# Opening of a fused FFT and feed-forward kernel: first sequence's loads on two queues, its stores and first reads on others

## Chip, core and metric

The kernel runs on one core of one Trainium2 chip. The metric is the device time of one execution in microseconds, the median of several runs. Before the change it is 2823.06 us (3 runs, 2822.7 to 2823.41).

## What is computed

The input x has 8 sequences of 3008 rows with 256 channels, in float32. Each sequence is transformed, mixed, soft-thresholded and transformed back; all 24064 rows then pass a gated feed-forward layer:

```python
X = np.fft.rfft(x, axis=1)
Yr = Xr @ w_r - Xi @ w_i + b_r
Yi = Xr @ w_i + Xi @ w_r + b_i
Y  = soft(Yr, 0.01) + 1j * soft(Yi, 0.01)      # sign(v) * max(|v| - 0.01, 0)
y  = np.fft.irfft(Y, n=3008, axis=1)
out = (sigmoid(y @ w_gate) * (y @ w_val)) @ w_out    # 256 -> 1536 -> 256
```

## The kernel before

The transform of 3008 = 47 x 64 points is made in two steps. Step A (`fwd_a`) takes 47-point transforms. A sequence is cut into 8 units `xf` of 96 rows x 1024 floats (384 KB); a unit is loaded (`load_a`), multiplied in two halves of 512 columns with the constant `fa_sb` (`product_a`, tile `pa`), copied from the PSUM bank back over the unit and stored (`store_a`) to a scratch tensor `zd` in DRAM. Of the two copies of a unit, ScalarE makes the first and VectorE the second while the sequence is 0 or 1. Step B (`load_b`, `fwd_b`) reads `zd` back in 12 pieces q of 256 KB (`zf`), and each piece needs rows of all 8 units, so none can be read before the last unit of its sequence has been stored. `fwd_b` multiplies it with a table `mf_sb` (`pb`), `mix4` multiplies with the mixing weights (`pm`), `inv_b` goes back with a table `mi_sb` (`pi`), and the result is stored to `vd`. The steps of three successive q are interlaced: round q makes `pb` of q, `pm` of q-1, `pi` of q-2.

Only sequence 0 is computed with nothing beside it; its opening is written out by hand (lines 853 to 914) under a manual schedule, so every engine takes its instructions in program order. Ahead of the first unit and again ahead of the first `pb`, TensorE runs matmuls on zeros (`keep_warm`, tile `warm`, L830): 13 and 10 of them. Between, step A runs for the 8 units of sequence 0 and for the first 4 (`EARLY`) of sequence 1. Later sequences are transformed beside the feed-forward layer, which fills most of the program.

All plain transfers of this opening are issued by SP (`nc.sync`), except the load of `fa_sb`, which ACT issues first; POOL (`nc.gpsimd`) issues the stores to `vd`. Transfers that SP and ACT issue take eight completion semaphores in turn, DMAHW0 to DMAHW7, in program order over both engines. A transfer that gets a semaphore a second time waits, on its issuing engine, until the transfer that held it before has landed. POOL's transfers have eight of their own (DMASW0 to DMASW7). Three PSUM banks hold `pa` and `pb`.

Of the kernel before, what the change touches and what calls it, by code (L numbers as in the profile page):

```python
# [19 lines left out]
R2, R1 = 47, 64  # L20
NK2 = 24
NQ = 2 * NK2
# [10 lines left out]

LAST_GAP, SIDE_GAP = 20, 3
PRE = 2
WARM = 13
WARM_Z, WARM_V = 10, 5
EARLY = 4
AT_FIRST = 3
NCONV = 7  # L40
# [69 lines left out]
def tile_fft_mix_ffn(ctx: ExitStack, tc, x, w_r, w_i, b_r, b_i, w_one, w_out, mf, mi, mis, fa, fb, out):  # L110
    nc = tc.nc
# [3 lines left out]
    XR = x.shape[2]  # L115
# [25 lines left out]
    def bank(name, tag="fft", bufs=FFT_BANKS):  # L141
        return (psf if tag == "fft" else psl).tile([P, 512], F32, tag=tag, bufs=bufs, name=name)
# [10 lines left out]
    zd = [tc.dram_tile([NQ, R1, D], F32, name=f"zd{b}") for b in range(B)]  # L153
# [4 lines left out]
    xv = x.rearrange("b u p (h c) -> b u p h c", c=D)  # L158
# [7 lines left out]
    def big(name):  # L166
        return p2.tile([P, 4, D], F32, tag="big", bufs=NBIG, name=name)

    def load_a(b, h):
        xf = p0.tile([P, 4, D], F32, name="xf0", bufs=R1 // 8) if b == 0 else big("xf")  # L170
        nc.sync.dma_start(xf[:XR], xv[b, h])
        held["x", b, h] = xf

    def product_a(xi, az, copy):
        pa = bank("pa")[:2 * NQ]
        nc.tensor.matmul(pa, fa_sb, xi, start=True, stop=True)  # L176
        copy(az, pa.rearrange("p (h c) -> p h c", h=2))  # L177

    def fwd_a(b, h):

        xf = held["x", b, h]
        for i in range(2):
            at = slice(2 * i, 2 * i + 2)
            product_a(xf[:2 * R2, at], xf[:2 * NQ, at], nc.vector.tensor_copy if b < 2 and i else nc.scalar.copy)

    def store_a(b, h, queue=nc.sync):
        queue.dma_start(zv[b][:, 4 * h:4 * h + 4], held.pop(("x", b, h))[:2 * NQ])

    def load_half(b, h):
        xf = r2k("xfh").bitcast(F32)  # L190
        nc.sync.dma_start(xf[:XR], xv[b, h // 2, :, h % 2 * 2:h % 2 * 2 + 2])
        held["xh", b, h] = xf
# [9 lines left out]
    def load_mf(q):  # L202
        t = p2.tile([P, 2, P], F32, name="mf_sb", bufs=NMF)
        nc.sync.dma_start(t, mf[2 * q:2 * q + 2].rearrange("q p k -> p q k"))
        return t
# [18 lines left out]
        nc.gpsimd.dma_start(md[2 * q:2 * q + 2].rearrange("q p a k -> p q a k"), t.bitcast(F32))  # L224
        kept.add(q)

    def load_b(b, q):
        zf = p2.tile([P, 2, D], F32, tag="ld", bufs=NLD, name="zf")
        nc.sync.dma_start(zf, zd[b][4 * q:4 * q + 4].rearrange("(q a) n c -> (a n) q c", q=2))
        held["z", b, q] = zf  # L230

    def fwd_b(b, q, m, full):
        zf = held.pop(("z", b, q))
        pb = bank("pb").rearrange("p (c q k) -> p c q k", c=CT, q=2)
        for i in range(2):
            for ct in range(CT):
                nc.tensor.matmul(pb[:, ct, i], zf[:, i, ct * P:(ct + 1) * P], m[:, i], start=True, stop=True)  # L237
        xh, xl = (p2.tile([P, CT, 3, 2 * R1], F32R, tag=t, name=t) for t in ("xsh", "xsl"))
        if full:

            xh, xl = (t.rearrange("p c s k -> p c (s k)").rearrange("p c (q k) -> p c q k", q=2) for t in (xh, xl))
            nc.scalar.copy(xh[:, :, :, 64:], pb)
            sub(xl[:, :, :, 64:], pb, xh[:, :, :, 64:])
            for t in (xh, xl):
                nc.scalar.mul(t[:, :, :, :64], t[:, :, :, 128:], -1.0)
        else:

            xf = p2.tile([P, CT, 3, 2, R1], F32, name="xsf", bufs=1)
            nc.scalar.copy(xf[:, :, 0:2].rearrange("p c t q k -> p c q t k"),
                           pb.rearrange("p c q (t k) -> p c q t k", t=2))  # L250
            nc.vector.tensor_add(xf[:, :, 2], xf[:, :, 0], xf[:, :, 1])
            flat = xf.rearrange("p c s q k -> p c s (q k)")
            nc.scalar.copy(xh, flat)
            sub(xl, flat, xh)
        held["xs", b, q] = xh, xl
# [490 lines left out]
    def load_mix():  # L746
        for w in (w_r, w_i):
            wf = f2k("wf")
            nc.sync.dma_start(wf, w.rearrange("(t p) d -> p t d", p=P))
            wfs.append(wf)  # L750

    def load_bias4():
        for i, v in enumerate((b_r, b_i)):
            nc.sync.dma_start(bias4[64 * i:64 * i + 64], v.rearrange("(o d) -> o d", o=1).broadcast_to([64, D]))

    def load_bias():
        for i, v in enumerate((b_r, b_i)):
            nc.sync.dma_start(bias_sb[:, i], v.rearrange("(o d) -> o d", o=1).broadcast_to([P, D]))

    def mix_weights():  # L760
        wi = p0.tile([P, CT, 2, D], F32R, tag="xf0", bufs=R1 // 8, name="wi_sb")
        nc.scalar.copy(wi[:, :, 0], wfs[1])
        sub(wi[:, :, 1], wfs[1], wi[:, :, 0])
        wd, wn = f2k("wd"), f2k("wn")
        sub(wd, wfs[1], wfs[0])
        nc.vector.scalar_tensor_tensor(wn, wfs[0], -1.0, wfs[1], op0=ALU.mult, op1=ALU.subtract)
        for i, w in enumerate((wfs[0], wd, wn)):
            nc.scalar.copy(w_sb[:, :, 0, i], w)
            sub(w_sb[:, :, 1, i], w, w_sb[:, :, 0, i])
        return wi  # L770
# [24 lines left out]
    def load_part():  # L795
        k, f = parts.pop(0)
        if len(parts) >= 3 * NF // 2 - NCONV:
            raw = p0.tile([P, 2, D, 2], U32, tag="xf0", bufs=R1 // 8, name="raw0")
        else:
            raw = p2.tile([P, 2, D, 2], U32, tag="big", bufs=NBIG, name="raw")  # L800
        nc.sync.dma_start(raw.rearrange("p i n w -> p (i n w)"), (w_out[f // 2] if k else w_one[f]).bitcast(U32))
        raws.append((k, f, raw))
# [24 lines left out]
    def keep_warm(o, l, r, n):  # L827

        for _ in range(n):
            nc.tensor.matmul(o, l, r, start=True, stop=True)  # L830

    keep_warm(bank("warm"), zero[:, :P], zero, WARM)
    tables = {}
# [5 lines left out]
    mfs, mis_ = {}, {}  # L839
# [13 lines left out]
    with tc.manual_schedule():  # L853
        for h in range(na):
            load_a(0, h)
        load_a(1, 0)
        for h in range(na):
            fwd_a(0, h)
            store_a(0, h)
            if h in (1, 3, 4):  # L860
                load_a(1, {1: 1, 3: 2, 4: 3}[h])
            if h == 2:
                load_mix()
        mfs[0] = load_mf(0)
        for q in range(2):
            load_b(0, q)
        mfs[1] = load_mf(1)
        load_bias4()
        load_part()
        mfs[2] = load_mf(2)  # L870
        for h in range(EARLY):
            fwd_a(1, h)
            if h == 1:
                wi_sb = mix_weights()
        keep_warm(bank("warm"), zero[:, :P], zero, WARM_Z)
        for q in range(NP + 2):
            if q + 2 < NP:
                load_b(0, q + 2)
            if 0 <= q - 1 < NP:
                mis_[q - 1] = load_mi(q - 1, True)  # L880
            if q < 2:
                for h in range(q * EARLY // 2, (q + 1) * EARLY // 2):
                    store_a(1, h)
            if q == 3:
                nc.sync.dma_start(fb_sb, fb)
                load_bias()
            if q % 2 and q <= NP:
                load_part()
            if q % 2 == 0 and 4 <= q < 4 + 2 * (na - EARLY):
                load_a(1, EARLY + q // 2 - 2)  # L890
            if q < NP:
                fwd_b(0, q, mfs[q], True)
            if q + 3 < NP:
                mfs[q + 3] = load_mf(q + 3)

            if q % 2:
                ops("sum word", 0)
                start_part(p0)
                ops("exp top", -1)
            elif q:  # L900
                ops("power mant", -1)
                if len(started) > 1:
                    ops("hi lo", 0)
                ops("one", -1)
            if q == 4:
                sub(bias_sb[:, 1], bias_sb[:, 1], bias_sb[:, 0])
            if 0 <= q - 1 < NP:
                mix4(0, q - 1)
            if q == NP + 1:

                fwd_a(1, EARLY)
                store_a(1, EARLY, nc.gpsimd)
            if 0 <= q - 2 < NP:
                inv_b(0, q - 2, mis_[q - 2], True)

        for bh in beside[:NR2K]:
            load_half(*bh)
        left = ["hi lo", "power mant one", "sum word", "hi lo"]
        for h in range(EARLY + 1, na):
            ops(left.pop(0), 0)  # L920
            fwd_a(1, h)
            store_a(1, h, nc.gpsimd)
        ops(left.pop(0), 0)
# [46 lines left out]
    n = len(a3) // 3  # L970
# [13 lines left out]
    for j in range(NF, len(ffn)):  # L984
        c, f = divmod(j, NF)
# [46 lines left out]
    with tc.manual_schedule():  # L1032
# [16 lines left out]
        n = NPR * NH  # L1049
# [36 lines left out]
```

## Time and profile before

| | |
|---|---|
| median of 3 runs | 2823.06 us |
| the profiled execution, its own time | 2821.45 us |
| its span, first to last instruction | 2819.6 us |
| TensorE (PE) busy | 2802.0 us, 99% |
| VectorE (DVE) / ScalarE (ACT) / GpSimd (POOL) busy | 74% / 46% / 25% |
| data moved by the 16 DMA engines | 241.01 MB, mean 85 GB/s |

The profiled execution has a span of 2819.6 us and a time of 2821.45 us, so 1.85 us lie outside of the span. PE is the matmul engine, PEld its weight loads. SPq, ACTq and POOLq are the sequencers that issue transfers. The 40 slices of the page show the DMA engines busy in the first two fifths of the program and hardly afterwards.

### The profile page before, as it was taken

What the parts mean: (1) busy time and instruction counts of PE and PEld (TensorE: products, weight loads), DVE (VectorE), ACT (ScalarE), POOL (GpSimd) and SP (SyncE); (2) the same over time, 40 slices, a digit from 0 to 9 for tenths busy, and PEclk for the clock granted to TensorE, in tenths of its full rate; (3) what the DMA queues carried; (4) which work ended last, traced back from release to release, by engine and by line L of the source; (5) the groups of instructions that cost most, each with busy time, mean ns of one, the idle gap of its engine ahead of it and who ended that gap; (6) DMA issues with size and microseconds to landing.
All of it is one profiled execution on the core that took longest, in us unless ns stands there. A gap on an engine that the chain in (4) does not pass through costs nothing.

```text
span 2819.6 us, 38247 instructions
## 1 busy us (share of the span) xinstructions
PE 2802.0 (99%) x13896; PEld 2307.9 (82%) x13896; DVE 2082.6 (74%) x3109; ACT 1309.8 (46%) x2276; POOL 711.7 (25%) x638
## 2 busy tenths in 40 slices
PE   9999999999999999999999999999999999999999
PEld 6778888888899887888888888888888888888887
DVE  5778778667787536777777777777777777777776
ACT  4664544544455444444444444444444444444443
POOL 0211010224100002333333333333333343333321
PEclk9999999999999999999999999999999999999999
DMA  9866545656554661000000000000000000000000
GB/s 295 265 214 190 172 138 156 200 180 191 163 156 144 185 182 36 30 15 16 30 31 24 7 31 31 31 16 15 31 30 16 15 30 31 30 1 30 30 16 16
DMA packets 173469, 241.01 MB, mean 85 GB/s; under 512 B 14592, under 2 KB 124896, under 8 KB 173280
## 3 DMA queue, kind: packets, MB, share of 16 engines
q1 hardware_dynamic: 163776, 214.93, 24.9%
q0 software_dynamic: 9408, 23.60, 2.5%
q8 instruction: 110, 1.80, 0.3%
q14 instruction: 79, 0.65, 0.1%
q10 hardware_dynamic: 96, 0.04, 0.0%
HBM read 134.17 MB, written 104.33 MB: 85 GB/s over the span
## 4 chain that ended last, share of the span: by engine, by line
PE 95%; DVE 2%; DMA 2%; ACT 0%; issue 0%; SPq 0%; DVEq 0%; ACTq 0%
PE pd L653 11%; PE pc L653 11%; PE pa L653 11%; PE po L630 8%; PE po L629 8%; PE po L628 8%; PE pm L271 6%; PE pb L653 5%; PE pia L340 4%; PE pa L176 3%; PE pb L237 3%; PE pg L395 2%; PE pg L397 2%; PE po L420 2%; PE pg L396 2%; PE po L421 2%
## 5 line engine op out<-in xcount | busy, mean ns | idle before, releaser
L630 PE MATMUL po<-hl,w 128*128 128x512 f32 x912 | 362.7, 398 | 0.0
L629 PE MATMUL po<-hh,w 128*128 128x512 f32 x912 | 361.7, 397 | 0.0
L628 PE MATMUL po<-hh,w 128*128 128x512 f32 x912 | 360.9, 396 | 0.0
L712 POOL TENSOR_TENSOR c<-c,c 128x512 f32<-128x512 f32 x114 | 147.7, 1296 | 833.5 <-DVE c L708 613.4
L653 PE MATMUL pc<-s,w1h 128*128 128x512 f32 x912 | 284.1, 393 | 1.4 <-DVE v L687 1.4
L653 PE MATMUL pa<-a,w1h 128*128 128x512 f32 x912 | 284.1, 393 | 0.0
L708 DVE TENSOR_TENSOR c<-u,pc 128x512 f32<-128x512 f32 x228 | 156.7, 687 | 114.7 <-PE pc L653 106.3
L683 DVE TENSOR_TENSOR u<-u,pb 128x512 f32<-128x512 f32 x228 | 155.3, 681 | 91.1 <-PE pb L653 64.1
L600 ACT CAST hh<-v 128x512 fp32r<-128x512 f32 x114 | 70.7, 620 | 306.0 <-DVE v L693 306.0
L630 PEld LDWEIGHTS po<-hl,w 128*128 128x128 f32 x912 | 171.5, 188 | 41.9
L628 PEld LDWEIGHTS po<-hh,w 128*128 128x128 f32 x912 | 172.1, 189 | 40.9
L629 PEld LDWEIGHTS po<-hh,w 128*128 128x128 f32 x912 | 171.1, 188 | 40.7
L653 PEld LDWEIGHTS pa<-a,w1h 128*128 128x128 f32 x912 | 171.2, 188 | 40.1
L653 PEld LDWEIGHTS pc<-s,w1h 128*128 128x128 f32 x912 | 170.9, 188 | 39.5 <-DVE v L687 2.3
L604 POOL TENSOR_TENSOR hl<-c,hh 128x512 fp32r<-128x512 f32 x114 | 152.6, 1338 | 186.1 <-ACT hh L600 186.1
L271 PE MATMUL pm<-w_sb,xsh 128*128 128x256 f32 x1008 | 189.4, 288 | 1.4 <-ACT xf L177 1.1
L653 PE MATMUL pc<-s,w1l 128*128 128x512 f32 x456 | 177.6, 389 | 0.0
L653 PE MATMUL pa<-a,w1l 128*128 128x512 f32 x456 | 177.0, 388 | 0.0
L685 DVE TENSOR_TENSOR v<-u,pd 128x512 f32<-128x512 f32 x228 | 156.8, 688 | 25.0 <-DVE u L683 0.9
L714 DVE TENSOR_TENSOR u<-u,pd 128x512 f32<-128x512 f32 x228 | 156.9, 688 | 24.4 <-DVE c L708 0.9
L687 DVE TENSOR_TENSOR v<-v,pc 128x512 f32<-128x512 f32 x228 | 156.6, 687 | 24.1 <-DVE v L685 0.5
L679 ACT COPY u<-pa 128x512 f32<-128x512 f32 x228 | 133.7, 586 | 81.6 <-PE pa L653 81.6
(166 smaller groups left out, 6739.6 us busy)
## 6 DMA issues: line engine op xcount, KB each, us to landing
zf<-zd SPq DMA_DIRECT2D x96, 256.0 KB, 3.5
vf<-vd SPq DMA_DIRECT2D x128, 192.0 KB, 3.2
out_dram<-ot SPq DMA_DIRECT2D x93, 256.0 KB, 2.2
vd<-vz SPq DMA_DIRECT2D x84, 256.0 KB, 2.9
ypair<-yd SPq DMA_DIRECT2D x19, 1024.0 KB, 5.0
yd<-yf SPq DMA_DIRECT2D x103, 188.0 KB, 3.1
xf<-in_x_dram SPq DMA_DIRECT2D x48, 384.0 KB, 4.2
zd<-xf SPq DMA_DIRECT2D x44, 384.0 KB, 3.6
```

The costliest lines, as they stand in the source:

```text
L271: nc.tensor.matmul(o, l, r, start=(i == 0), stop=(i == len(mms) - 1))
L604: sub_(hl, h, hh)
L628: nc.tensor.matmul(o, wh, hh, start=(f == 0), stop=False)
L629: nc.tensor.matmul(o, wl, hh, start=False, stop=False)
L630: nc.tensor.matmul(o, wh, hl, start=False, stop=(f == NF - 1))
L653: nc.tensor.matmul(o, l, r, start=not more and l is wh and r is xh, stop=l is wl, skip_group_check=more)
L683: add(u, u, b)
L685: add(v, u, d)
L687: add(v, v, c)
L708: add(c12, u, c)
L712: nc.gpsimd.tensor_mul(c12, g12, c12)
L714: add(u, u, d)
```

## The change

Sequence 0's units are now loaded as two halves of 192 KB (512 columns each), the first issued by SP, the second by ACT. Of the two copies of a unit of sequence 0, VectorE now makes the first and ScalarE the second; sequence 1 keeps its order. The stores of sequence 0's units are issued by ACT, each right behind ACT's copy of that unit. The first two reads `zf` are issued by POOL. The loads of sequence 1's units 1, 2, 3 stand after units 1, 4, 6 of sequence 0 (before 1, 3, 4), and the first `mf` table after unit 5 (before after unit 7). The fourth unit of sequence 1 passes step A after the first `pb` instead of ahead of the second group of `warm`, and the four stores of sequence 1 stand one in each of rounds 0 to 3 instead of two in each of rounds 0 and 1. The `warm` groups have 10 and 5 matmuls.

```diff
-WARM = 13
-WARM_Z, WARM_V = 10, 5
+WARM = 10
+WARM_Z, WARM_V = 5, 5
...
     def load_a(b, h):
         xf = p0.tile([P, 4, D], F32, name="xf0", bufs=R1 // 8) if b == 0 else big("xf")
-        nc.sync.dma_start(xf[:XR], xv[b, h])
+        if b == 0:
+            for i, queue in enumerate((nc.sync, nc.scalar)):
+                queue.dma_start(xf[:XR, 2 * i:2 * i + 2], xv[b, h, :, 2 * i:2 * i + 2])
+        else:
+            nc.sync.dma_start(xf[:XR], xv[b, h])
...
-            product_a(xf[:2 * R2, at], xf[:2 * NQ, at], nc.vector.tensor_copy if b < 2 and i else nc.scalar.copy)
+            product_a(xf[:2 * R2, at], xf[:2 * NQ, at], nc.vector.tensor_copy if b < 2 and i == b else nc.scalar.copy)
...
-    def load_b(b, q):
+    def load_b(b, q, queue=nc.sync):
...
-        nc.sync.dma_start(zf, zd[b][4 * q:4 * q + 4].rearrange("(q a) n c -> (a n) q c", q=2))
+        queue.dma_start(zf, zd[b][4 * q:4 * q + 4].rearrange("(q a) n c -> (a n) q c", q=2))
...
-            store_a(0, h)
-            if h in (1, 3, 4):
-                load_a(1, {1: 1, 3: 2, 4: 3}[h])
+            store_a(0, h, nc.scalar)
+            if h in (1, 4, 6):
+                load_a(1, {1: 1, 4: 2, 6: 3}[h])
...
-        mfs[0] = load_mf(0)
+            if h == 5:
+                mfs[0] = load_mf(0)
         for q in range(2):
-            load_b(0, q)
+            load_b(0, q, nc.gpsimd)
...
-        for h in range(EARLY):
+        for h in range(EARLY - 1):
             fwd_a(1, h)
...
-            if q < 2:
-                for h in range(q * EARLY // 2, (q + 1) * EARLY // 2):
-                    store_a(1, h)
+            if q < EARLY:
+                store_a(1, q)
...
             if q < NP:
                 fwd_b(0, q, mfs[q], True)
+            if q == 0:
+                fwd_a(1, EARLY - 1)
```

ACT's rows at the start of the program, before. `fa_sb` is step A's constant, `xf_123` unit 0 and `xf_125` unit 1 of sequence 0; what stands behind "waits" are semaphores, DMAHW those of transfers:

```order
1 L151 DMA fa_sb<-in_fa_dram 94x96
2 L177 ACT_TABLE_LOAD [waits DMAHW1_49]
3 L177 COPY xf_123<-pa 96x512 [waits PE_49]
4 L177 COPY xf_125<-pa 96x512 [waits DMAHW2_49,PE_49]
5 L177 COPY xf_127<-pa 96x512 [waits DMAHW3_49,PE_49]
```

ACT's rows at the same place now, where `xf_120`, `xf_123`, `xf_126`, `xf_129` are units 0 to 3 and `zd_77` is sequence 0's scratch tensor:

```order
3 L173 DMA xf_123<-in_x_dram 96x512
4 L173 DMA xf_126<-in_x_dram 96x512
5 L173 DMA xf_129<-in_x_dram 96x512 [waits DMAHW0_49]
6 L173 DMA xf_132<-in_x_dram 96x512 [waits DMAHW2_49]
7 L173 DMA xf_135<-in_x_dram 96x512 [waits DMAHW4_49]
8 L173 DMA xf_138<-in_x_dram 96x512 [waits DMAHW6_49]
9 L173 DMA xf_141<-in_x_dram 96x512 [waits DMAHW0_49]
10 L181 ACT_TABLE_LOAD
11 L181 COPY xf_120<-pa 96x512 [waits PE_49]
12 L191 DMA zd_77<-xf_120 96x1024 [waits DMAHW3_49,DVE_49,Activation_49]
13 L181 COPY xf_123<-pa 96x512 [waits PE_49]
14 L191 DMA zd_77<-xf_123 96x1024 [waits DMAHW6_49,DVE_49,Activation_49]
```

Eight loads now stand ahead of ACT's first copy, five of them with a wait for an earlier transfer, and a store stands behind each copy. In the last load DMAHW0 is that of unit 3's second half.

SP's rows around the last stores of sequence 0, before (`xf<-in_x_dram` are units of sequence 1, `wf` the mixing weights):

```order
13 L187 DMA zd_77<-xf_127 96x1024 [waits DMAHW5_49,DVE_49,Activation_49]
14 L749 DMA wf<-in_w_r_dram 128x2x256 [waits DMAHW6_49]
15 L749 DMA wf<-in_w_i_dram 128x2x256 [waits DMAHW7_49]
16 L187 DMA zd_77<-xf_129 96x1024 [waits DMAHW0_49,DVE_49,Activation_49]
17 L171 DMA xf<-in_x_dram 96x1024 [waits DMAHW1_49]
18 L187 DMA zd_77<-xf_131 96x1024 [waits DMAHW2_49,DVE_49,Activation_49]
19 L171 DMA xf<-in_x_dram 96x1024 [waits DMAHW3_49]
20 L187 DMA zd_77<-xf_133 96x1024 [waits DMAHW4_49,DVE_49,Activation_49]
21 L187 DMA zd_77<-xf_135 96x1024 [waits DMAHW5_49,DVE_49,Activation_49]
22 L187 DMA zd_77<-xf_137 96x1024 [waits DMAHW6_49,DVE_49,Activation_49]
23 L204 DMA mf_sb<-in_mf_dram 128x2x128 [waits DMAHW7_49]
24 L229 DMA zf<-zd_77 128x2x256 [waits DMAHW5_49,DMAHW4_49,DMAHW6_49,DMAHW2_49,DMAHW0_49]
```

SP's rows there now; `raw_222` is a piece of the feed-forward weights, and the `zf` in row 21 is the third one:

```order
10 L175 DMA xf<-in_x_dram 96x1024 [waits DMAHW2_49]
11 L753 DMA wf<-in_w_r_dram 128x2x256 [waits DMAHW4_49]
12 L753 DMA wf<-in_w_i_dram 128x2x256 [waits DMAHW5_49]
13 L175 DMA xf<-in_x_dram 96x1024 [waits DMAHW7_49]
14 L208 DMA mf_sb<-in_mf_dram 128x2x128 [waits DMAHW0_49]
15 L175 DMA xf<-in_x_dram 96x1024 [waits DMAHW2_49]
16 L208 DMA mf_sb<-in_mf_dram 128x2x128 [waits DMAHW3_49]
17 L758 DMA bias_98<-in_b_r_dram 64x256 [waits DMAHW4_49]
18 L758 DMA bias_98<-in_b_i_dram 64x256 [waits DMAHW6_49]
19 L805 DMA raw_222<-in_w_one_dram 128x1024 [waits DMAHW7_49,DVE_49,Activation_49]
20 L208 DMA mf_sb<-in_mf_dram 128x2x128 [waits DMAHW1_49]
21 L233 DMA zf<-zd_77 128x2x256 [waits DMAHW4_49,DMAHW3_49,DMAHW5_49,DMAHW2_49,DMAHW0_49]
```

SP's list has lost the stores: loads that stood behind a store, or behind the first `zf`, now stand ahead of it. By the order of issue the semaphores pair the stores on ACT with these loads: the store of unit 2 waits for the landing of sequence 1's unit 0, that of unit 3 for `w_i`, of unit 4 for the first `mf`, of unit 5 for sequence 1's unit 3, of unit 6 for the second `mf`, and that of unit 7 for `b_r` (row 17). Behind the rounds of the opening the five engines have the same instructions in the same order as before.

## Rows read from the trace of the kernel before

**Rows 1.** Busy time by stretch of the span, with granted clock and DMA.
```profile
core 0: us, PE busy (x) PEld busy (x) DVE busy (x) ACT busy (x) POOL busy (x), PEclk, DMA share, GB/s
0.00:40.00 40.00, 34.81 (x120) 18.84 (x121) 15.71 (x26) 13.87 (x24) 0.20 (x4) 1.00 0.91 281
40.00:80.00 40.00, 39.63 (x311) 38.48 (x311) 33.99 (x59) 25.32 (x47) 6.00 (x8) 1.00 0.98 300
120.00:2819.60 2699.60, 2689.41 (x13293) 2224.49 (x13291) 2004.52 (x2975) 1247.18 (x2163) 696.02 (x610) 1.00 0.25 77
```
**Rows 2.** PE in order of time: start, us, instruction, idle before and its releaser.
```profile
1.46 4.98 PE L830 MATMUL warm<-zero 128*128 128x512 f32 x13 [1.46 <-DVE ebias L838]
6.28 17.49 PE L176 MATMUL pa<-xf,fa_sb 94*96 94x512 f32 x40
...
28.10 2.77 PE L830 MATMUL warm<-zero 128*128 128x512 f32 x10
31.88 1.13 PE L237 MATMUL pb<-mf_sb,zf 128*128 128x128 f32 x8 [1.02 <-issue]
...
38.97 1.13 PE L237 MATMUL pb<-mf_sb,zf 128*128 128x128 f32 x8 [1.52 <-DMA zf<-zd]
...
47.90 1.10 PE L305 MATMUL pi<-yc,mi_sb 128*128 128x256 f32 x4 [0.37 <-DMA mi_sb<-in_mi_dram]
```
**Rows 3.** The chain that ended last, 0 to 140 us: start, us, what.
```profile
21.47 7.49 DMA zd<-xf
...
32.83 6.00 DMA zf<-zd
...
49.00 0.89 PE pb L237 x8
49.89 2.84 PE pm L293 x24
```
**Rows 4.** SP's queue in order of time: start, us, transfers issued.
```profile
0.74 5.91 SPq L171 DMA_DIRECT2D xf<-in_x_dram  x9
...
29.04 0.89 SPq L229 DMA_DIRECT2D zf<-zd  x2
```
**Rows 5.** SP's waits, 0 to 60 us: total, times, longest.
```profile
SPq L171 <- DMA fa_sb<-in_fa_dram: 1.9, 1, 1.9
```
**Rows 6.** ACT in order of time, first rows; columns as in rows 2.
```profile
5.18 1.28 ACT L177 ACT_TABLE_LOAD   x1 [5.18 <-DMA xf<-in_x_dram]
7.33 0.58 ACT L177 COPY xf<-pa 96x512 f32<-96x512 f32 x1 [0.87 <-PE pa L176]
```
**Rows 7.** The transfers of the first 28.5 us in sum.
```profile
DMA packets 3118, 8.54 MB, mean 300 GB/s; under 512 B 461, under 2 KB 1198, under 8 KB 3118
```
**Rows 8.** Four stretches; columns as in rows 1, DMA rate last.
```profile
5.00:14.00 9.00, 9.00 (x24) 3.85 (x23) 2.56 (x4) 3.61 (x5) 0.00 (x0) 1.00 1.05 263
16.00:28.00 12.00, 11.28 (x27) 3.71 (x25) 6.94 (x11) 6.18 (x11) 0.00 (x0) 1.00 1.03 388
...
88.00:91.00 3.00, 3.00 (x15) 2.04 (x14) 2.81 (x6) 1.27 (x2) 0.42 (x1) 1.00 0.94 326
104.00:109.00 5.00, 4.38 (x26) 3.57 (x26) 2.32 (x5) 2.77 (x5) 0.00 (x0) 1.00 1.02 397
```
**Rows 9.** DMA queues, 104 to 109 us: packets, MB, share of 16 engines.
```profile
q1 hardware_dynamic: 504, 1.00, 53.4%
q0 software_dynamic: 303, 0.98, 48.6%
```
**Rows 10.** POOL's stores to vd, 40 to 100 us: ns min/median/max, times, landing.
```profile
L313 POOL DMA_DIRECT2D vd<-vz x12: 725/725/902, 44.7 to 94.4; - x12
...
DMA to landing us min/median/max: 2.6/5.4/7.7
```
**Rows 11.** Warm matmuls on PE, 2.1 to 5 us and 29.2 to 30.4 us: ns, starts.
```profile
L830 PE MATMUL warm<-zero x8: 628/628/795, 1.5 to 4.6; 128*128 128x512 f32 x8
...
L830 PE MATMUL warm<-zero x7: 389/389/394, 28.9 to 30.2; 128*128 128x512 f32 x7
```

## The prediction

> **What bounds the kernel now.** First I read the stretches. Behind 120 us TensorE is busy for 2689.41 of 2699.60 us, and the instructions there don't change; so the change can only move the moment at which that work begins [rows 1]. From 40 to 80 us PE is busy for 39.63 of 40 us too. The loss lies in the first 40 us, where PE is busy for 34.81 us, warm matmuls among them, while the DMA engines are at 0.91 [rows 1].
>
> Then I read PE in order of time. The reader is to see four losses: `pa` begins at 6.28 us; after step A there are 2.77 us of `warm` and 1.02 us of nothing, until the first `pb` at 31.88; the third `pb` waits 1.52 us for `zf` and begins at 38.97; a `pi` waits 0.37 us for a table [rows 2]. From there PE runs without a gap worth naming, so what counts is the time at which the third `pb` starts, plus the 0.37 us.
>
> The chain says what sets it: the store of the last unit, issued at 21.47 us, takes 7.49 us and lands at 28.96; then SP issues the first two `zf` [rows 3, 4]. The third `zf` is issued at 32.83 and takes 6.00 us, behind other loads [rows 3]. So the opening hangs on DMA: how many bytes stand ahead of the last store, and how fast they move. In 28.5 us 8.54 MB moved, 300 GB/s [rows 7]. That rate has two parts: from 5 to 14 us, units of x alone, 263 GB/s; from 16 to 28 us, loads and stores mixed, 388 GB/s; the DMA share is 1.0 in both [rows 8].
>
> **The change part by part.** The sum is made against the profiled execution's own 2821.45 us, 1.61 us under the median of 2823.06.
>
> *Warm matmuls.* At full pace one follows another in 0.22 us (seven from 28.9 to 30.2) [rows 11]. Three fewer let `pa` begin at 6.28 - 0.66 = 5.62 us, if its data are there. `fa` landed at about 5.85: SP's nine issues end at 6.65, the last two took some 0.4 us each, and the wait for `fa` ended right before them [rows 4, 5]. So `pa` gains 0.4 to 0.66 us; it is not on the path, since the last store is late for other reasons (below), and counts 0. Five fewer ahead of `pb` lie in the wait for `zf` and count 0 too. The price if the cover fails: after idling, the eight first warm matmuls took 628 ns where later ones took 389, 8 x 0.24 = 1.9 us [rows 11]. I take 0, since gaps of 1.02 and 1.52 us left the two `pb` groups behind them at 1.13 us each [rows 2].
>
> *ACT as a queue.* An issue costs (5.91 - 1.9) / 9 = 0.45 us [rows 4, 5]. Eight of them would delay ACT by 3.6 us, but the fourth waits for `fa` (5.85 us) and the eighth for the landing of the fourth. Unit 3 is 1.5 MB into the stream; at 263 GB/s, from about 2 us, with 1.5 to 2 us to land, that is 9.5 to 10 us. Then comes the table load, 1.28 us, so ACT's first copy comes at about 11.5 instead of 7.33 us [rows 6]. PE makes five products of 0.87 us (17.49 / 20) until 10 us [rows 2], and then stalls some 2 us for a bank that ACT has not emptied. This lies beside the x loads, which run until 14 us anyway, and counts 0 as long as DMA sets the last store.
>
> *Bytes ahead of the last store.* Before: 12 units of x and 8 stores at 384 KB, `wf` 512 KB, `fa` 35 KB, together 8.42 MB. Now the store of unit 7 can't be issued before `b_r` lands, and ahead of that stand two `mf` (128 KB each) and `b_r` (64 KB): 0.33 MB more, 0.85 us at 388 GB/s. Up to 0.72 MB more (`b_i`, `raw`, a third `mf`), issued by SP without a store before them, can share the engines with the last stores: 2.7 us in all. Between 0.85 and 2.7 I take 1.8.
>
> *Two queues for x.* The 3.15 MB of sequence 0 took 12.0 us at 263 GB/s. Halves of a unit, in rows of 2 KB and almost alone, moved at 326 GB/s from 88 to 91 us; two queues, half loads and half stores, at 397 from 104 to 109 [rows 8, 9]. That makes 12.0, 9.6 or 7.9 us: a gain from 0 to 4.1. The nearest row is the 326, but there SP alone issued the loads; I take half of its 2.4 us, 1.2. The Trainium skill (DMA: Bandwidth & Descriptors, section Rules for kernel authors) speaks against this term: spreading transfers over SP, ACT and GpSimd doesn't help bandwidth, since all run on the same 16 DMA engines and interleave. The 397 of two queues beside the 388 of one agrees with it for mixed traffic; for loads alone no row here decides. By that rule this term is 0 and the sum 1.2 us higher.
>
> *Stores in ACT's order.* A store waiting for its semaphore now holds up ACT's next copy, and so the bank that PE needs. The store of unit 5 leaves when sequence 1's unit 3 has landed. Behind it two more rounds of copy (0.58) and issue (0.45) follow, about as long as a store's own transfer (0.39 MB at 388 GB/s, 1.0 us). I take a bubble of 0.5 us, within 0 to 1.5.
>
> The last store then lands at 28.96 + 1.8 - 1.2 + 0.5 = 30.1 us.
>
> *First two `zf` by POOL.* Before: from issue at 29.04 to `pb` at 31.88, 2.84 us [rows 2, 4]. POOL takes 0.73 to 0.90 us to issue 256 KB, and its stores land 2.6 us after the start in quiet, 5.4 in the median [rows 10]. The third `zf`, now issued by SP at the same moment, shares the engines. I take 3.6 us, 0.75 more; bounds -0.2 and +2.5.
>
> *From first to third `pb`.* Before, 38.97 - 31.88 = 7.09 us. Now: `pb` 0.89, the fourth unit of sequence 1 (two products, 1.74), `pb` 0.89, `pm` 2.84 [rows 2, 3], together 6.36, if the third `zf` is there; it no longer stands behind `raw` and the biases. -0.75, with +0.9 if it is late. The wait of 0.37 us ahead of `pi` goes as well, since that table is asked for earlier relative to PE: -0.37, or 0.
>
> Sum: 1.8 - 1.2 + 0.5 + 0.75 - 0.75 - 0.37 = +0.73 us, from 2821.45 to 2822.2 in a profiled execution; on the median, 2823.06 + 0.73 = 2823.8 us. All lower ends together give 0.85 - 4.1 + 0 - 0.2 - 0.75 - 0.37 = -4.6 us, all upper ends 2.7 - 0 + 1.5 + 2.5 + 0.9 + 0 = +7.6 us.
>
> **The rivals.**
>
> *The two queues pay in full.* If loads alone go at the 397 GB/s of two queues, sequence 0 has landed at about 11 instead of 15 us; ACT's first copy comes near 9.5; the last store lands near 26, PE idles less, and the time is about 2823.06 - 4 = 2819.1. For it: 263 GB/s is far under what the same engines moved later at the same share of 1.0 [rows 8]. Against it: PE's own 16 products take 14 us and end near 20 at the earliest, and more bytes stand ahead of the last store.
>
> *ACT's queue becomes the bound.* Place: the stores of units 2 to 7, each held until a load of SP's queue has landed, with ACT's copies, PE's banks and the next stores behind it. Price: no gain from the queues, 2.7 us of bytes, a 1.5 us bubble, a late `zf` (+0.75 to +2.5) less 0.75 to 1.1: about +5 us, 2828. It decides from the point at which the last store lands after 31.5 us. For it: the waits in the order; before, a store waited only for loads issued long before. Against it: in the chain before, the engines were never idle until 28 us, so a held store gives its time to a load that has to be moved anyway.
>
> *The fewer warm matmuls cost.* If the longer stalls slow what follows, 1.9 us are added to the forecast; it lies within the range and is counted with the second rival.
>
> **How the numbers follow.** Forecast (-1.5 to +2.5 us): 0.55; two queues pay: 0.25; ACT the bound: 0.20. The likeliest gives 2823.8 us. Forecasts of both signs hold much of the chance, so the likeliest one's own range is 2821.6 to 2825.6; the range for 8 in 10 takes in most of both rivals, 2819.3 to 2827.8. About what a measurement of this kernel can tell from no change is 0.2%, 5.6 us. Only the tails beyond the rivals' own prices reach that: 0.06 faster and 0.06 slower, 0.88 within.
>
> **What would show it.** Right: the DMA rate over the first 14 us above 263 but under 330 GB/s; ACT's first copy after 10 us and a PE stall of about 2 us ahead of the sixth product; the last store of `zd` landing at 30 us, the first `pb` at 33 to 34, the third at about 39.7 with no wait for `zf` ahead of it, and from there every row of PE at a constant shift. Wrong: a last store that lands under 28 or over 32 us; a first copy of ACT at 8 us; `pm` beginning late because the mixing weights, which ACT now casts behind its last store, are not ready; or PE rows behind 120 us whose shift is not that of the third `pb`.

## The result and the profile after

The changed kernel takes 2836.91 us (median, 2835.29 to 2839.07), the kernel before 2822.88 in the same runs: the ratio is 1.0049, with an interval of 1.0037 to 1.0061. It is slower, by 14 us (0.5%); forecast was +0.7, within 2819.3 to 2827.8. The profiled execution took 2837.03 us, 15.6 more than that of before.

First the stretches of the changed kernel; columns as in [rows 1].

```profile
0.00:40.00 40.00, 35.25 (x50) 12.58 (x50) 7.01 (x12) 8.13 (x13) 1.84 (x6) 0.67 0.87 260
...
6.00:13.00 7.00, 4.86 (x12) 1.43 (x10) 2.06 (x3) 1.86 (x2) 0.00 (x0) 1.00 1.07 258
14.00:47.00 33.00, 31.38 (x41) 10.44 (x40) 9.10 (x14) 7.39 (x13) 1.64 (x2) 0.50 0.70 228
48.00:60.00 12.00, 12.00 (x92) 10.82 (x91) 8.05 (x14) 7.62 (x15) 0.73 (x1) 1.00 0.82 251
```

In [rows 1] PE does 120 matmuls in the first 40 us, here 50, and is just as busy: 35.25 against 34.81 us. Busy time hides the loss; the clock column shows it. TensorE's granted clock is at its upper level (2.4 GHz) until 13 us, at the lower one (1.2 GHz) from 14 to 47 us, and at the upper one again from 48.

PE in order of time, the changed kernel; columns as in [rows 2].

```profile
1.46 4.63 PE L834 MATMUL warm<-zero 128*128 128x512 f32 x10 [1.46 <-DVE ebias L842]
5.89 4.93 PE L180 MATMUL pa<-xf,fa_sb 94*96 94x512 f32 x10
12.96 22.16 PE L180 MATMUL pa<-xf,fa_sb 94*96 94x512 f32 x26 [2.14 <-ACT xf L181]
...
43.15 3.12 PE L834 MATMUL warm<-zero 128*128 128x512 f32 x5
46.33 1.69 PE L241 MATMUL pb<-mf_sb,zf 128*128 128x128 f32 x8
...
53.30 1.06 PE L241 MATMUL pb<-mf_sb,zf 128*128 128x128 f32 x8
```

Ten passes (five products) take 4.93 us; then PE waits 2.14 us for ACT; the next 26 passes take 22.16 us, 0.85 each instead of the 0.44 of [rows 2]. The third `pb` starts at 53.30 instead of 38.97 us. That is 14.3 us of the 15.6; the first matmul of the next stage (tile `po`) is 14.7 us late, and the end 15.6. The prediction expected one constant shift behind the third `pb`; 1.3 us more arise there. The medians differ by 14.0 us only, and executions of the kernel before lie from 2820.86 to 2826.34 us (those beside e9), so the 1.3 may be spread.

The chain that ended last, the changed kernel, 0 to 140 us; columns as in [rows 3].

```profile
4.56 6.10 DMA xf<-in_x_dram
...
10.68 0.32 ACTq L173
...
11.03 0.44 ACT L181
...
12.33 0.59 ACT xf L181
...
12.96 22.18 PE pa L180 x26
...
46.33 1.69 PE pb L241 x8
```

Before, the chain ran over the last store and the read of it [rows 3]. Now it goes from a load of x to ACT's last issue, through ACT's table load and first copy, into PE's slow passes.

ACT in order of time, the changed kernel, the rows that matter; columns as in [rows 6], ACTq is ACT's issuing.

```profile
1.30 9.70 ACTq L173 DMA_DIRECT2D xf<-in_x_dram  x8
11.03 1.28 ACT L181 ACT_TABLE_LOAD   x1 [11.03 <-DMA xf<-in_x_dram]
12.33 0.58 ACT L181 COPY xf<-pa 96x512 f32<-96x512 f32 x1
...
18.09 0.58 ACT L181 COPY xf<-pa 96x512 f32<-96x512 f32 x1 [1.67 <-PE pa L180]
23.06 0.31 ACTq L191 DMA_DIRECT2D zd<-xf  x1
...
32.36 0.31 ACTq L191 DMA_DIRECT2D zd<-xf  x1
```

The first copy is at 12.33 us, against 7.33 in [rows 6]. The store of unit 3, whose copy is done at 18.67 us, leaves at 23.06: it waits for `w_i`, which lands at 22.96. The last store leaves at 32.36 and lands at 35.35, before 28.95.

SP in order of time, the changed kernel; columns as in [rows 4].

```profile
20.58 0.55 SPq L758 DMA_DIRECT2D bias<-in_b_r_dram  x1
22.10 0.47 SPq L758 DMA_DIRECT2D bias<-in_b_i_dram  x1
24.44 0.35 SPq L805 DMA_DIRECT2D raw<-in_w_one_dram  x1
24.84 0.43 SPq L208 DMA_DIRECT2D mf_sb<-in_mf_dram  x1
```

POOL in order of time, the changed kernel:

```profile
36.15 1.64 POOL L233 DMA_DIRECT2D zf<-zd  x2 [35.71 <-DMA zd<-xf]
```

Biases, `raw` and a third `mf` go out from 20 to 25 us, between the stores; before, they stood behind the `zf`. POOL's two `zf` land at 41.94 and 42.63 us. PE is not done with step A by then, so their lateness doesn't show here.

### The profile page after: what moved, and what is told of

It reads as the page before. It is cut to its first block, busy times and chain, and to the rows that moved or that the text cites. A ratio compares the mean times of both kernels' runs of the same rounds, so it can differ in the third digit from the quotient of the medians.

```text
span 2835.2 us, 38242 instructions
## 1 busy us (share of the span) xinstructions
PE 2816.5 (99%) x13888; PEld 2310.5 (81%) x13888; DVE 2082.8 (73%) x3109; ACT 1310.0 (46%) x2276; POOL 712.3 (25%) x640
## 4 chain that ended last, share of the span: by engine, by line
PE 96%; DVE 2%; DMA 1%; ACT 0%; issue 0%; SPq 0%; ACTq 0%; DVEq 0%
PE pd L657 11%; PE pc L657 11%; PE pa L657 11%; PE po L634 8%; PE po L633 8%; PE po L632 8%; PE pm L275 6%; PE pb L657 5%; PE pia L344 4%; PE pa L180 4%; PE pb L241 3%; PE pg L399 2%; PE pg L401 2%; PE pg L400 2%; PE po L424 2%; PE po L425 2%
```

## The experiments

The theory: the held loads on ACT make PE stall, the stall takes the clock, and step A at half the clock is the loss. The rivals: the transfers themselves (late stores, POOL's read), the fewer warm matmuls, or the orders. "Third `pb`" is its start in the profiled execution, 38.97 before and 53.30 after.

**Filling the stall** (e1, e2). To the changed kernel, nine warm matmuls between the halves of unit 2; in e2 13 more in unit 6 (`FILL = {2: 9, 6: 13}`).

```
+FILL = {2: 9}
+            if b == 0 and i and h in FILL:
+                keep_warm(bank("warm", "l1", L1_BANKS), zero[:, :P], zero, FILL[h])
```

> The changed kernel with nine matmuls on zeros between the two products of sequence 0's unit 2, in a bank that nothing else uses there: 9 x 0.22 us fill the 2.14 us in which PE waits for ACT's first copy; transfers and their order stay. Theory 1 (the clock): the granted clock fell to 0.5 at 13.3 us because PE stood idle from 10.8 to 13.0; filled, the clock stays at 1.0 past 13.3 us. If the later holds of ACT (the store of unit 3 waits for w_i until 23 us) make a second stall, the clock falls there, at 18 to 22 us, and only part comes back: 2825 to 2832; without one 2824 +- 2. Rival 1 (transfers): bytes ahead of the last store and held stores set the end, the clock only makes PE slower where it waits anyway; the last store lands at 35 us as in the changed kernel and the time stays within 2 us of 2836.9. Rival 2 (ten warm matmuls are too few): nothing changes at the start, the clock falls all the same, 2836 to 2839.

> As the run with one group of fill, and thirteen more matmuls on zeros between the two products of unit 6, where ACT's held stores should make PE wait for a bank once PE runs at full pace. Theory 1: the clock stays at 1.0 through the opening; the last store lands at 28 to 31 us, the first pb starts at 32 to 34.5, and the time is 2822 to 2826. Rival 1: last store at 35 us, time within 2 us of 2836.9. Rival 2: as before, 2836 to 2839.

e1: 2835.17 us, ratio 1.0045 [1.003, 1.006]. The time misses the range of the theory and lies within 2 us of 2836.9, as rival 1 expected; what speaks for the theory is the clock. Behind the filled stall it stays at its upper level; it falls behind a second stall, 2.97 us long, and is at 0.50 from 26 to 42 us. PE of e1 in order of time:

```profile
24.23 7.79 PE L181 MATMUL pa<-xf,fa_sb 94*96 94x512 f32 x10 [2.97 <-DMA xf<-in_x_dram]
```

e2: 2833.79 us, 1.0039 [1.0025, 1.0053], outside all three ranges. PE of e2 in order of time:

```profile
39.19 2.05 PE L244 MATMUL pb<-mf_sb,zf 128*128 128x128 f32 x8 [5.17 <-issue]
...
48.69 1.06 PE L244 MATMUL pb<-mf_sb,zf 128*128 128x128 f32 x8
```

Two stretches of e2; columns as in [rows 1]:

```profile
5.00:38.00 33.00, 27.54 (x73) 11.45 (x72) 11.09 (x17) 9.84 (x16) 1.64 (x2) 1.00 0.97 292
39.00:45.00 6.00, 5.81 (x15) 3.61 (x16) 1.00 (x2) 1.95 (x4) 0.00 (x0) 0.50 0.36 112
```

Step A is done at full clock and ends by 33 us, but the third `pb` gains only 4.6 us. The last store still lands at 33.57, the read through POOL makes PE idle for 5.17 us, and this idle time takes the clock in its turn. So the clock of step A is not the whole answer in this kernel: behind it stood a second loss, covered until now.

**The reads back on SP** (e5): e2 with `load_b(0, q)` in place of `load_b(0, q, nc.gpsimd)`.

> The changed kernel with both groups of fill and with the first two zf read by SP as before the change. With fill alone the clock held through step A, yet the third pb began at 48.69 us (before 38.97, changed kernel 53.30): last store at 33.57, first pb 5.6 us later. Theory 2 (three separate prices: the clock, a last store that is late because ACT issues loads and held stores, and POOL's slower read): with SP's read the first pb follows the last store within 3.2 us, the idle time behind the warm group shrinks under 3 us, and the third pb begins at 41.5 to 44.5; 2826 to 2830. Rival (the read is late because it shares the engines with the third zf and a store): the first pb still comes over 5 us after the last store, time within 2 us of 2833.8.

2825.78 us, 1.0009 [0.9999, 1.0019]: not told apart from before, and 0.2 us under the range of the theory. PE of e5 in order of time:

```profile
33.02 1.13 PE L244 MATMUL pb<-mf_sb,zf 128*128 128x128 f32 x8 [0.50 <-DMA zf<-zd]
...
40.05 1.13 PE L244 MATMUL pb<-mf_sb,zf 128*128 128x128 f32 x8 [0.45 <-DMA zf<-zd]
```

SP of e5 in order of time:

```profile
18.17 0.33 SPq L176 DMA_DIRECT2D xf<-in_x_dram  x1
30.13 0.89 SPq L236 DMA_DIRECT2D zf<-zd  x2
31.07 0.46 SPq L211 DMA_DIRECT2D mf_sb<-in_mf_dram  x1
```

With its `zf` in SP's order, SP stands still from 18.5 to 30.13 us, and a table, the biases, `raw` and another table wait behind it. The stores also came to wait for other transfers. The store of unit 3 in e2:

```profile
22.68 0.31 ACTq L194 DMA_DIRECT2D zd<-xf  x1
```

And in e5:

```profile
19.39 0.31 ACTq L194 DMA_DIRECT2D zd<-xf  x1
```

In e2 it is held for `w_i`, which lands at 22.58 us; in e5 it leaves before `w_i` has landed (22.56). It is the same with the store of unit 5: in e2 it is held for sequence 1's unit 3, and the chain that ended last runs through it:

```profile
18.32 7.73 DMA xf<-in_x_dram
...
26.15 0.31 ACTq L194
...
26.50 0.59 ACT xf L182
```

In e5 that store leaves at 22.66 us, though sequence 1's unit 3 lands later than in e2 (27.18 against 26.05). So it is not earlier landings that set the stores free in e5, but that they no longer wait for these loads. The last store leaves at 26.70 us (e2: 29.17) and lands at 30.05 (33.57). So from e2 to e5 the third `pb` gains 8.6 us: 3.5 in the last store (2.5 of it in its issue), 2.7 from there to the first `pb` (2.97 against 5.62), 2.5 from the first to the third `pb`, at full clock again.

**All loads by SP** (e3: halves both by `nc.sync`; e6: the `zf` by SP as well).

```
-            for i, queue in enumerate((nc.sync, nc.scalar)):
+            for i, queue in enumerate((nc.sync, nc.sync)):
```

> The changed kernel with both halves of sequence 0's units issued by SP; ACT keeps the stores. Theory 1: ACT's first copy comes at about 7.5 us, the stall of 2.14 us at 10.8 us goes; if ACT's held stores then stall PE for more than 2 us later on, the clock falls there, some 5 to 10 us later than in the changed kernel: 2824 to 2832. Rival 1: the held stores and the bytes are what costs, so 2834 to 2838. Rival 2: unchanged start of ten warm matmuls, 2836 to 2839.

> The changed kernel with all loads and the first two zf issued by SP; what is left of the change is the stores by ACT, the order of sequence 1's loads and units, and the shorter warm groups. With SP's loads alone the last store landed at 29.38 us, the first pb began at 35.35 and the third at 43.97, 2828.77 us. Theory 2: the first pb comes at 31.5 to 32.8 us, the third at 38.5 to 41; 2821.5 to 2825. Rival 1 (stores by ACT and bytes ahead of the last store cost): the third pb stays at 43 us or later, 2827 or more.

e3: 2828.77 us, 1.0021 [1.0012, 1.003]; ACT's first copy at 7.74 us, the last store at 29.38, the third `pb` at 43.97. The clock falls in e3 too, at 26 us, not behind one stall of more than 2 us but behind two of 0.78. e6: 2824.65 us, 1.0008 [0.9998, 1.0017]; third `pb` at 41.22, last store at 30.23. Taking ACT out of the loads gives back 8 us; the reads on POOL are most of what is left. In e3, as in e2, SP sends the second table, the biases, `raw` and the third table early (21.66 to 27.09 us), while in e6 they wait behind the `zf`; yet the last store lands 0.85 us earlier in e3. So what SP sends early does not by itself make the last store late.

**One part of the change alone, on the kernel before** (e8: the loads in halves on SP and ACT; e7: the first two `zf` by POOL; e10: `store_a(0, h, nc.scalar)`; e11: only the orders and the split of the copies).

> The kernel before with sequence 0's units loaded as halves by SP and ACT and nothing else: stores and reads by SP, 13 and 10 warm matmuls, copies in the old order. Theory 2: ACT's first copy comes at 11 to 13 us behind its held loads, PE stalls 2 us or more, the granted clock falls to 0.5 in the stall or behind it, and the last store lands 2 to 8 us later; 2828 to 2838. Rival (only the stores on ACT, held by SP's loads, make the last store late): the last store lands at 28 to 30 us, the clock holds, 2821.5 to 2825.

> The kernel before with the first two zf read by POOL and nothing else. Theory 2: the first pb begins 2 to 4 us later than at 31.88 us, the third pb is moved by as much or somewhat less, since it waits 1.52 us for its own zf anyway; 2823.5 to 2827. Rival (POOL's issue is hidden): the first pb at 31.8 to 32.5, 2821.5 to 2823.5.

> The kernel before, with the eight stores of sequence 0 issued by ACT and nothing else changed. Theory (the split loads alone delay ACT): the first copy comes at 7 to 8 us, PE has no stall over 1 us before 20 us, the last store lands within 1.5 us of 28.95 and the time is 2822 to 2825 us. Rival (the stores, held for loads in ACT's order, stall PE and take the clock as well): a stall of over 1.5 us in step A, the granted clock at 0.5 behind it, and at least 2828 us.

> Only the orders of the changed kernel: the loads of sequence 1's units and of the first table at other places, its fourth unit behind the first pb, its stores one a round, its copies split the other way round; all transfers by SP, whole units, 13 and 10 warm matmuls as before. Theory (the orders take the 1.52 us wait ahead of the third pb and leave the rest): the last store lands within 1 us of 28.95, the third pb begins 0.5 to 1.5 us before 38.97 and the time is 2821 to 2823 us. Rival (the orders cost as well, through bytes ahead of the last store): the last store lands at 30 us or later and the time is 2824 us or more.

e8: 2838.14 us, 1.0055 [1.004, 1.007]. PE of e8 in order of time:

```profile
1.46 5.91 PE L834 MATMUL warm<-zero 128*128 128x512 f32 x13 [1.46 <-DVE ebias L842]
7.17 3.91 PE L180 MATMUL pa<-xf,fa_sb 94*96 94x512 f32 x8
12.96 33.16 PE L180 MATMUL pa<-xf,fa_sb 94*96 94x512 f32 x40 [1.88 <-ACT xf L181]
```

A stretch of e8; columns as in [rows 1]:

```profile
14.00:48.00 34.00, 34.00 (x44) 12.28 (x43) 10.39 (x16) 7.98 (x14) 0.00 (x0) 0.50 0.76 233
```

The split alone gives the whole loss (third `pb` at 54.65), with all 13 warm matmuls, before's stores and before's orders: neither the fewer warm matmuls nor the orders are needed for it. The time is 0.1 us above the theory's range.

e7: 2826.99 us, 1.0016 [1.0007, 1.0026]. PE of e7 in order of time:

```profile
35.89 3.75 PE L237 MATMUL pb<-mf_sb,zf 128*128 128x128 f32 x16 [4.35 <-issue]
42.90 1.05 PE L237 MATMUL pb<-mf_sb,zf 128*128 128x128 f32 x8
```

POOL of e7 in order of time:

```profile
29.65 1.64 POOL L229 DMA_DIRECT2D zf<-zd  x2 [29.20 <-DMA bias<-in_b_i_dram]
```

The last store lands at 29.03, as before; the `zf` land at 35.80 and 36.50, 6.2 and 6.0 us after their issue, where the second of SP's took 3.1 before. The third `pb` is 3.9 us late. From 29.10 to 30.44 us SP now issues the third `zf` and two stores of sequence 1 beside them; no run tells whether POOL's own way or this company makes the reads slow.

e10: 2823.51 us, 1.0002 [0.9993, 1.0011], and e11: 2824.08 us, 1.0004 [0.9995, 1.0013]: not told apart from before. In e10 the last store lands 1.8 us later, at 30.76; the theory expected 1.5 at most; the third `pb` starts at 40.84. In e11 it lands at 29.65 and the third `pb` starts at 40.62, 1.7 us later and not earlier, and the time is at the rival's 2824. PE of e11 in order of time:

```profile
32.51 1.22 PE L237 MATMUL pb<-mf_sb,zf 128*128 128x128 f32 x8 [3.00 <-issue]
33.52 3.53 PE L176 MATMUL pa<-xf,fa_sb 94*96 94x512 f32 x4
```

The 1.52 us of waiting ahead of the third `pb` are gone, but with a unit less ahead of the first `pb` PE idles there for 3.00 us instead of 1.02. The clock falls, and the four passes behind take 3.53 us, where they take 1.88 in e5.

**The stall alone** (e4: 15 copies, e9: 20). No transfer of the kernel before is changed; ACT copies zeros ahead of its first copy.

```
+        idle = f2k("idle")
+        for _ in range(20):
+            nc.scalar.copy(idle, zero.bitcast(F32).rearrange("p (a d) -> p a d", a=2))
```

> The kernel before, with nothing of the change, and 15 copies of 128x512 zeros on ACT ahead of its first copy of the opening (about 0.58 us each), so that PE stalls once for some 2 us while 13 warm matmuls and all transfers stay as they were. Theory 1: the granted clock falls to 0.5 within a microsecond or so of the stall and stays there for some 30 us; step A takes 1.7 us a product; 2832 to 2839. Rival 1: PE loses the stall alone and the transfers hide part of it: 2822.5 to 2826. Rival 2: thirteen warm matmuls hold the clock: 2822.5 to 2826.

> The kernel before, with 20 idle copies of zeros ahead of ACT's first copy: every transfer is issued as before, and only PE stalls. With 15 such copies PE waited 0.78 and 0.30 us; 5 more, at some 0.5 us, should make one stall of 2 to 3 us behind the fifth product, like the 2.14 us of the changed kernel. Theory (the stall takes the clock): the granted clock falls to 0.5 behind the stall and stays there for 20 us or more, step A takes twice as long, the first pb begins at 40 us or later and the time is 2830 us or more. Rival (the transfers are what is late, the clock only follows): the clock stays at 1.0 or is back within 10 us, the last store lands by 30.5 us and the time is at most 2825 us.

e4 was inconclusive: PE waited 0.78 and 0.30 us, too little, the clock stayed at 1.00 in the profiled execution, and the time is 2823.09 us, 1.0006 [0.9997, 1.0015]. But one of its ten executions took 2835.45 us at a mean granted clock of 0.994, which is that of the changed kernel (0.993 to 0.996); the other nine took 2822.18 to 2824.43 at 0.999 to 1.000. That execution has no trace, but its time and clock are what theory 1 expects. e9: 2839.96 us, 1.0059 [1.0047, 1.0072]. PE of e9 in order of time:

```profile
10.75 1.10 PE L176 MATMUL pa<-xf,fa_sb 94*96 94x512 f32 x2 [0.78 <-DVE xf L177]
16.10 32.74 PE L176 MATMUL pa<-xf,fa_sb 94*96 94x512 f32 x38 [4.25 <-ACT xf L177]
```

A stretch of e9; columns as in [rows 1]:

```profile
15.00:52.00 37.00, 35.90 (x46) 13.61 (x47) 10.39 (x16) 9.40 (x17) 0.00 (x0) 0.50 0.69 209
```

The stall was longer than meant (4.25 us). With each transfer on its old queue, in its old order, the clock falls and the whole loss is there (third `pb` at 57.81, 4.5 us later than in the changed kernel). This decides for the theory: a late ACT is enough.

**Warm matmuls behind the stall** (e12): the changed kernel with `FILL = {3: 12}`, so inside the slow stretch.

> The changed kernel, with 12 matmuls of zeros between the two halves of unit 3, so behind the stall and in the stretch at granted clock 0.5 (in the changed kernel 13.3 to 47.5 us). Theory (what keeps the clock low is what PE runs: the products of step A hold a clock but don't bring it back, while a row of warm matmuls does): at the lower clock the 12 take some 5 us, the granted clock is back at 1.0 by 25 us, the passes behind it take half as long, the third pb begins at 47 to 51 us instead of 53.30 and the time is 2830 to 2835 us, the late stores and POOL's transfers being left. Rival (the chip keeps the clock low for a time, whatever PE runs): the granted clock stays at 0.5 until 40 us or later, the 12 matmuls come on top and the time is 2838 us or more.

2833.98 us, 1.004 [1.0026, 1.0054]. PE of e12 in order of time:

```profile
12.79 2.81 PE L181 MATMUL pa<-xf,fa_sb 94*96 94x512 f32 x4 [1.76 <-ACT xf L182]
14.61 4.54 PE L837 MATMUL warm<-zero 128*128 128x512 f32 x12
18.99 10.23 PE L181 MATMUL pa<-xf,fa_sb 94*96 94x512 f32 x22
```

Two stretches of e12; columns as in [rows 1]:

```profile
14.00:17.00 3.00, 3.00 (x6) 1.66 (x5) 0.69 (x1) 0.58 (x1) 0.00 (x0) 0.50 1.04 262
17.50:37.00 19.50, 16.65 (x43) 6.42 (x41) 8.33 (x13) 6.82 (x12) 1.64 (x2) 1.00 0.92 310
```

The same stall, and the clock falls; during the warm matmuls it comes back, 30 us earlier than in the changed kernel, and 22 passes take 10.23 us. The rival (the clock stays low until 40 us or later, whatever PE runs) is out. The clock falls a second time, behind 4.23 us of idling ahead of the first `pb` (0.50 from 38 to 46 us); the third `pb` starts at 49.78. Clock, third `pb` and time came as the theory expected.

None of the versions is faster than the kernel before.

## Why the prediction was wrong, point by point

The account, by the start of the third `pb`: from before to e5 +1.1 us (stores on ACT, orders, shorter warm groups, split loads with their stalls filled), from e5 to e2 +8.6 (the `zf` on POOL, nothing else), from e2 to the changed kernel +4.6 (the fills gone, and with them the clock in step A); together 14.3. The start of the third `pb` is not the whole time: the profiled execution of e5 is 2.8 us longer than that of before, and no run shows what makes the other 1.7. Alone on the kernel before, the split is worth 15.7 (e8) and POOL 3.9 (e7). They don't add: in the changed kernel the slow step A ends at 44.1 us, behind the landing of the late reads (41.94 and 42.63).

*ACT as a queue: the step that failed.* The delay itself was forecast to within a microsecond: first copy at about 11.5 us (12.33), a PE stall of some 2 us ahead of the sixth product (2.14). Its price was not: it "counts 0 as long as DMA sets the last store". The stall itself did lie beside the loads; what it did to the clock behind it did not. Behind it the granted clock was 0.50 from 14 to 47 us, and step A, which before ended 3.8 us ahead of the first `pb` (28.10 against 31.88, [rows 2]), became the bound: a term put at 0 is alone worth 15.7 us of the third `pb` (e8).

*Warm matmuls.* Here a PE that is slow after idling was considered and priced at 1.9 us, the eight slow warm matmuls of [rows 11], and taken as 0 because idle gaps of 1.02 and 1.52 us had left `pb` at full pace [rows 2]. Both numbers were read too narrowly: the gaps were shorter than the 2.14 us to which the change leads, and the price has no reason to end after eight matmuls. Behind the stall 34 passes of `pa` stand ahead of the first `pb`; at the measured 0.85 instead of 0.44 us that is 14 us, and, as an estimate from the ratio of 628 to 389 ns in [rows 11], it would have been 34 x 0.44 x 0.61 = 9 us. That bound should have stood in the sum.

*Two queues for x.* Taken as -1.2, bounds 0 and -4.1; it is 0. From 6 to 13 us the changed kernel moves 258 GB/s, before 263 [rows 8]. The Trainium skill's rule cited in the prediction (DMA: Bandwidth & Descriptors, section Rules for kernel authors) held for loads alone, too.

*Bytes ahead of the last store, and the bubble.* Forecast 30.1 us for the last store; 35.35 measured, and still 33.57 with the clock held (e2). The term that was too small is that of the stores in ACT's order, taken as 0.5 us and at most 1.5. The prediction had the mechanism, down to the store of unit 5 that waits for sequence 1's unit 3; in e2 the held stores make the last one leave 2.5 us later than in e5, where the same loads no longer hold them. Another 1.0 us lies in the transfer itself (4.40 us against 3.35), to which the bytes that SP sends early may add; the taken 1.8 us for bytes is not shown by any run, and in e3 such bytes cost the last store nothing.

*First two `zf` by POOL.* Taken as +0.75, at most 2.5; alone it makes the third `pb` 3.9 us late (e7), and none of that lies in the last store, which lands as before. POOL's transfers landed 6.0 and 6.2 us after issue, nearer to the 5.4 and 7.7 of [rows 10] than to the 2.6 that I leaned on. And the idle time, 4.35 us, took the clock for the `pb` behind it (3.75 us for 16 passes; 2.13 in e4, where the clock held).

*From first to third `pb`.* Taken as 6.36 us; 6.97 in the changed kernel, 7.03 in e5, before 7.09. The gain of 0.75 is 0.1 at most; in e5 the third still waited 0.45 us for its `zf`. The 0.37 us of `pi` did go.

*The rivals.* "ACT's queue becomes the bound" named the place and its sign, and its point of decision (a last store after 31.5 us) was met; its price of 5 us lacked the clock. "The two queues pay in full" needed 397 GB/s, and 258 were measured. "The fewer warm matmuls cost" is not needed for the loss, which e8 has with all 13 and 10; no run has the fewer ones alone.

## What to carry to other kernels

A stall that other work hides can still cost, through the clock of what follows: where it is longer than stalls that the trace shows to be harmless, price it with all the PE work behind it at the lower level, up to the next stretch known to run at the upper one. An engine that copies results out of PSUM shouldn't have to issue loads that are held for earlier transfers ahead of its copies. And when a transfer moves to another queue, read anew which transfers the others wait for: that can change for transfers that nobody touched.

## What the runs showed that I had not expected

- A single wait of 1.88 us (e8) or 2.14 us put the granted clock to 0.50 for over 30 us, with PE busy throughout (34.00 of 34 us in e8). The Trainium skill (TensorE: Matmul & The Clock Gate, section Part 1: The HAM clock gate (the "warmup" mystery)) calls the low level the default and says that activity releases it. These traces disagree with that for the passes of step A: 40 of them, back to back, did not bring the upper level back (e8), while 12 warm matmuls did (e12).
- It isn't only the instruction: in e11 the clock, fallen after 3.00 us of idling, came back while four passes of `pa` ran between two `pb` (0.50 from 33.5 to 36.8 us, then 1.05 us for the next `pb`). Nor is the length of the stall all: 0.78 and 1.08 us left the clock alone (e6), and so did 0.78 and 0.30 (e4), but it fell behind two of 0.78 us in e3. Which mix of work and waiting brings it down or back is open.
- Moving two reads to another queue changed which transfers the stores of unit 3 and later wait for, although neither the stores nor those transfers were touched (the store of unit 3 left at 22.68 us in e2, at 19.39 in e5).
